# Windowed attention and a routed feed-forward: query tiles made of half blocks j and j+4

## The chip, the cores and the metric

One core of a Trainium2 chip runs the whole program. The metric is the device time of one execution in microseconds (us); the time before is the median of three runs, and one further execution was profiled.

## The reference, cut to what matters

Eight batches, eight heads, 576 positions, head dimension 64, all in float32. Each position looks at itself and the 127 positions before it, with a bias that grows with distance at a slope of the head's own. The attention's output goes, as 4608 rows of 512, through a mixture of eight experts of which each row uses two.

```python
scores = scale * np.matmul(q, k.transpose(0, 1, 3, 2))
rel = pos[:, None] - pos[None, :]
mask = (rel >= 0) & (rel < window)          # window = 128
scores = np.where(mask, scores + bias[None], -1000000000.0)
attn = np.exp(scores - np.max(scores, axis=-1, keepdims=True))
attn = attn / (np.sum(attn, axis=-1, keepdims=True) + 1e-09)
x = np.matmul(attn, v)                      # then rows (B * S, H * D)
...
noisy_logits = x @ w_gate + np.log1p(np.exp(x @ w_noise)) * noise
top2 = np.argpartition(-noisy_logits, 2, axis=1)[:, :2]
...
h = np.maximum(x[mask] @ w1[e], 0.0)
out[mask] += top2_w[mask, k, None] * (h @ w2[e])
```

## The kernel before

The program has two stretches. In the first, some 235 us, the attention of 32 pairs of heads (eight batches, four pairs each) is worked through, the rows are routed to experts, and the first expert's weights are made ready. In the second, the experts' two matrix products run on TensorE almost without a break, each as three float16 products of high and low halves.

A pair of heads is worked in units. Unit 0 takes query blocks 0 and 1 (of 128 rows), unit 1 takes blocks 2 and 3, and a third unit takes the half block 4 of two pairs at once. For each unit `unit` issues, one after the other, the following steps.

- `scores` on TensorE: in four quadrants of 64 by 64, the keys that a half block of 64 rows can see. They go to two PSUM banks of the ring `sb` (two such pairs of banks).
- `top` on VectorE: a row sees 128 keys that lie in two neighbouring key blocks. Since exactly one of the two keys at distance 128 is inside the window, `copy_predicated` (line 543) folds the two blocks of columns into one of 128, by the mask `own_key`. Block 0 has no block before it, so unit 0 folds 128 columns a head and unit 1 folds 256. Then one custom instruction for each block and head (line 535) adds the bias, writes `p` and the row's extreme `nm`.
- `soft` on ScalarE: the exponential (line 559), with the row sums.
- `trans` on TensorE (line 572): four transposes of 128 by 128 into one bank of the ring `tb`, against the identity; `evac` copies that bank to `pT` (line 274 on ScalarE, 278 on VectorE, whichever the planner takes).
- `split` on GpSimd (lines 592 and 593) undoes the fold in `pT` by two selections.

When both units of a pair are there, `weigh` (line 608) multiplies `pT` with the values into one bank of the ring `ob`, and `weighed` copies it to `xu`. When a batch is complete, `row_major` transposes `xu` back (line 754), divides by the row sums (line 757) and stores rows of `x` (line 762); `gate` and `route` find the experts and, in two large comparisons (line 886), the places. Lines 1381 to 1387 scale gathered rows for the first expert, lines 274, 276 and 1280 split its weights into high and low halves, and line 1416 is its first product. Line 531 and line 617 are scores and weighing of the third unit.

The order on each engine is no order of the source. Each step is a strand of a small simulation (`Order`) that runs when the program is built: it takes the step with the lowest rank whose inputs are there, charges it an assumed time, and so writes down each engine's queue. The constants at the top (`STAGE`, `LATE`, `TOP`, `WEIGHTS` and the others) are these ranks and assumed times; a copy that either of two engines could do goes to the one that is first free by them. On the chip each engine then runs its queue strictly in that order and waits on semaphores.

## Time and profile before

| | |
|---|---|
| median of three runs (lowest to highest) | 1017.89 us (1011.57 to 1019.82) |
| profiled execution, its own time | 1015.87 us |
| span in that profile, first to last instruction | 1014.1 us |
| TensorE busy | 963.3 us, 95% of the span |
| VectorE busy | 841.5 us, 83% |
| ScalarE busy | 562.2 us, 55% |
| GpSimd busy | 385.2 us, 38% |

The times of single steps come from the profiled execution. Its time is 1.8 us more than its span, and 2.0 us less than the median. Shares of the whole span mix the two stretches, so they have to be read stretch by stretch.

### The profile page before, as it was taken

How to read it: one execution, taken by the hardware profiler on the slowest of the kernel's cores; microseconds unless marked ns; L12 is line 12 of the kernel's file. 1: busy time of each engine (PE TensorE's matmuls, PEld its weight loads, DVE VectorE, ACT ScalarE, POOL GpSimd, SP SyncE). 2: the span in 40 equal slices, each digit the busy share in tenths (PEclk: the TensorE clock that was granted, in tenths of full speed). 3: DMA queues.
4: the chain of work that ended last, by engine and by line, in shares of the span. 5: the costliest groups of instructions: out<-in, count | busy, mean ns of one | idle time of the engine just before them, and what ended most of it. 6: DMA issues, size and time to landing. Idle time of an engine off the chain costs nothing. (4 is left out here: it accounts for less than half of the span.)

```text
span 1014.1 us, 24481 instructions
## 1 busy us (share of the span) xinstructions
PE 963.3 (95%) x8656; PEld 664.4 (66%) x8656; DVE 841.5 (83%) x2786; ACT 562.2 (55%) x1491; POOL 385.2 (38%) x572
## 2 busy tenths in 40 slices
PE   8999999979999999999999999899999999999996
PEld 5766666646555866686677567666766676667663
DVE  8999999998558989878999898769877897898530
ACT  8997797842136545445544556465556463554422
POOL 3557675864335122421343223232323231241103
PEclk9999999989999999999999999999999999999999
DMA  9887889643499999597868888769797896878113
GB/s 336 306 275 234 295 301 320 198 108 105 106 206 241 226 214 175 131 199 219 152 146 185 214 156 179 159 194 200 122 225 195 172 176 197 171 156 154 26 21 51
DMA packets 236333, 188.84 MB, mean 186 GB/s; under 512 B 147056, under 2 KB 190352, under 8 KB 236208
## 3 DMA queue, kind: packets, MB, share of 16 engines
q1 hardware_dynamic: 218864, 148.31, 56.6%
q0 software_dynamic: 17344, 38.94, 20.5%
q8 instruction: 69, 1.13, 0.5%
q14 instruction: 56, 0.46, 0.1%
HBM read 116.24 MB, written 40.71 MB: 155 GB/s over the span
## 5 line engine op out<-in xcount | busy, mean ns | idle before, releaser
L1677 POOL DMA_INDIRECT out_dram<-yo,ix x69 | 121.8, 1765 | 250.2 <-ACT yo L274 144.9
L1573 PEld LDWEIGHTS <-hh 128*128 128x128 f16 x896 | 87.3, 98 | 83.5
L1541 ACT ACTIVATE hh<-c 128x512 f16<-128x512 f32 (+1 forms) x103 | 53.4, 528 | 114.3 <-DVE c L1511 108.8
L1541 ACT ACTIVATE hh<-bank 128x256 f16<-128x256 f32 (+8 forms) x121 | 42.4, 352 | 130.2 <-PE bank L1416 61.3
L1290 POOL DMA_INDIRECT xg<-xs_dram,ix x34 | 41.7, 1225 | 182.0 <-DVE ix L1037 60.7
L1573 PE MATMUL bank<-w2ha,hh 128*128 128x512 f16 x288 | 109.2, 379 | 0.0
L1573 PE MATMUL bank<-w2la,hh 128*128 128x512 f16 x288 | 109.2, 379 | 0.0
L1573 PE MATMUL bank<-w2ha,hl 128*128 128x512 f16 x288 | 109.2, 379 | 0.0
L1442 PEld LDWEIGHTS <-wth 128*128 128x128 f16 x896 | 87.3, 98 | 25.0 <-issue 6.0
L559 ACT ACTIVATE p<-p,nm 128x128 f32<-128x128 f32 x256 | 99.5, 402 | 2.1 <-DVE nm L535 1.9
L1573 PEld LDWEIGHTS <-hl 128*128 128x128 f16 x448 | 43.8, 98 | 52.8
L1502 DVE TENSOR_TENSOR c<-bank,c 128x512 f32<-128x512 f32 x56 | 38.3, 684 | 41.3 <-PE bank L1442 40.7
L274 ACT ACTIVATE c<-bank 128x256 f32<-128x256 f32 x97 | 36.0, 379 | 58.3 <-PE bank L1442 53.3
L535 DVE CUSTOM_DVE_ANT_0 p<-bank,bias 128x128 f32<-128x128 f32 x288 | 66.7, 282 | 0.1
L1442 PE MATMUL bank<-xhw,wth 128*128 128x256 f16 x224 | 61.0, 272 | 4.3 <-DVE c L1502 2.8
L1290 POOL DMA_INDIRECT xp<-xs_dram,ix x35 | 38.4, 1096 | 66.5 <-issue 24.4
L592 POOL TENSOR_SCALAR_AFFINE_SELECT pT<-pT 128x256 f32<-128x256 f32 (+1 forms) x80 | 44.9, 562 | 44.8 <-ACT pT L274 36.8
L514 PE MATMUL bank<-qk 64*64 64x192 f32 (+1 forms) x1024 | 55.2, 330 | 6.7 <-DVE raw L355 4.6
L1442 PE MATMUL bank<-xhe,wth 128*128 128x256 f16 x224 | 61.1, 273 | 0.0
L1442 PE MATMUL bank<-xhe,wtl 128*128 128x256 f16 x224 | 61.1, 273 | 0.0
L1442 PE MATMUL bank<-xle,wth 128*128 128x256 f16 x224 | 61.1, 273 | 0.0
L1442 PE MATMUL bank<-xhw,wtl 128*128 128x256 f16 x224 | 61.0, 272 | 0.0
(339 smaller groups left out, 3162.0 us busy)
## 6 DMA issues: line engine op xcount, KB each, us to landing
raw<-in_w_dram SPq DMA_DIRECT2D x144, 256.0 KB
mraw<-in_w_dram SPq DMA_DIRECT2D x56, 512.0 KB
qk<-in_qk_dram SPq DMA_DIRECT2D x32, 576.0 KB
vraw<-in_v_dram SPq DMA_DIRECT2D x16, 640.0 KB
out_dram<-xg SPq DMA_DIRECT2D x10, 1024.0 KB
xs_dram<-x SPq DMA_DIRECT2D x32, 256.0 KB
out_dram<-yo,ix POOLq DMA_INDIRECT x69
xs_dram<-x SPq DMA_DIRECT2D x8, 128.0 KB
```

Of the source, the lines that this page charges most:

```text
L274: nc.scalar.activation(o, i, AF.Copy, **kw)
L514: nc.tensor.matmul(s[h][a:a + 64, o + first_:o + first_ + c_], qk[half, i * 128 + a:i * 128 + a + 64], qk[half, QW + k0 + first_:QW + k0 + ...
L535: nc.vector.tensor_tensor_reduce(out=o, in0=i, in1=by, scale=-0.125, scalar=3.0e38, op0=OP.add, op1=OP.min, accum_out=m)
L559: nc.scalar.activation(pv, pv, AF.Exp, bias=nm[:, z, h:h + 1], scale=-1.0, accum_out=den[:, i, 2 * g + h:2 * g + h + 1])
L592: nc.gpsimd.affine_select(b, a, pattern, OP.is_ge, nothing, base=0, channel_multiplier=-1)
L1290: nc.gpsimd.indirect_dma_start(out=o, out_offset=None, in_=xs[0:blk.rows], in_offset=bass.IndirectOffsetOnAxis(ap=blk.at[0:r, j:j + 1], ax ...
L1442: nc.tensor.matmul(t, wp[:, at + kc], xp[:, 2 * o + kc], start=not add and kc + z == 0, stop=kc + z == 3, skip_group_check=add)
L1502: yield dve(0.6, rank - MIDDLE, lambda: nc.vector.tensor_tensor(both, y, both, op=OP.add))
L1541: nc.scalar.activation(o, i, AF.Relu)
L1573: nc.tensor.matmul(blk.y[j], h[:, cs], wp, start=a == 0 and z + m == 0, stop=a == 3 and z + m == 3)
L1677: ins = nc.gpsimd.indirect_dma_start(out=out, out_offset=bass.IndirectOffsetOnAxis(ap=blk.ix[0:r, j:j + 1], axis=0), in_=t[0:r], in_offset ...
```

## The change

A query tile now holds two half blocks of 64 rows: half block j on partitions 0 to 63 and half block j+4 on partitions 64 to 127, for j from 0 to 3. Unit 0 takes tiles 0 and 1, unit 1 tiles 2 and 3; the third unit is unchanged. Each half block sees three half blocks of keys, of which only the first and the last share a place, so the fold is 64 columns a tile and head: 128 columns a head in both units. The bias has three ranges of columns in one tile of 320 instead of two tiles of 128 by head.

A unit no longer transposes by itself. `turning` waits for the exponentials of both units of a pair and takes two banks at once. It issues 16 transposes that read 64 partitions each, alternately the lower and the upper half, the lower half's into one bank and the upper half's into the other; so each bank comes out as two consecutive query blocks of 128, as `weigh` wants them. The buffers `p` of both units are freed together. `pT` has two buffers of a whole pair, and one small one for the third unit, where there were four.

The ring `tb` gets a third bank, and the ring `ob` keeps one. Because a tile's halves lie 256 rows apart, the store of `x` and of the gates becomes two transfers of 64 rows. The two tiles of the comparisons exist once instead of twice. All ranks and some assumed times have other values, so every queue is written anew.

On TensorE in the course of the attention, before: single units' transposes (line 572) stand between other work, one bank each. `p` and `pT` are the buffers named above, `vraw` the values, `qk` queries and keys.

```order
L514 MATMUL bank_69<-qk_80 64x192
L572 MATMUL bank_72<-ident,p_85 128x128 x4
L531 MATMUL bank_66<-qk_79 64x192
...
L608 MATMUL bank_70<-pT_97,vraw_84 64x256 x2
L608 MATMUL bank_70<-pT_97,vraw_84 64x128 x2
L608 MATMUL bank_70<-pT_98,vraw_84 64x256 x2
L608 MATMUL bank_70<-pT_98,vraw_84 64x128 x4
L617 MATMUL bank_71<-pT_99,vraw_84 64x64 x8
L572 MATMUL bank_73<-ident,p_86 128x128 x4
L572 MATMUL bank_72<-ident,p_87 128x128 x4
L514 MATMUL bank_68<-qk_81 64x128
```

After, at the like place (transposes are line 576, weighing line 613, scores line 523, the third unit's transposes line 580): the two units `p_87` and `p_88` are turned in one run of 16, alternating between two banks.

```order
L523 MATMUL bank_69<-qk_79 64x192
L613 MATMUL bank_70<-pT_96,vraw_84 64x4x64 x2
...
L613 MATMUL bank_70<-pT_96,vraw_84 64x2x64 x4
L576 MATMUL bank_72<-ident,p_87 128x64
L576 MATMUL bank_73<-ident,p_87 128x64
...
L576 MATMUL bank_72<-ident,p_88 128x64
L576 MATMUL bank_73<-ident,p_88 128x64
...
L576 MATMUL bank_72<-ident,p_87 128x64
...
L576 MATMUL bank_72<-ident,p_88 128x64
L576 MATMUL bank_73<-ident,p_88 128x64
L580 MATMUL bank_71<-ident,p_89 128x128 x2
L523 MATMUL bank_66<-qk_80 64x192
```

The transposes of a pair have moved together, behind the second unit's exponentials, and each takes half the columns.

On ScalarE, pairs five and six, before: copies of `pT` (line 274) stand between the exponentials (559, and 565 for the third unit), and so do the squares for the weights' sizes (line 1246).

```order
L274 ACTIVATE pT_96<-bank_73 128x4x128
L565 ACTIVATE p_89,denl_107<-p_89,nm_93 128x128 x2
L559 ACTIVATE p_85,den_105<-p_85,nm_94 128x128 x4
L274 ACTIVATE pT_97<-bank_72 128x2x128
L559 ACTIVATE p_86,den_105<-p_86,nm_95 128x128 x4
L559 ACTIVATE p_87,den_105<-p_87,nm_90 128x128 x4
L274 ACTIVATE pT_99<-bank_72 128x4x128
L559 ACTIVATE p_88,den_105<-p_88,nm_91 128x128 x4
L274 ACTIVATE pT_96<-bank_73 128x2x256
L1246 ACTIVATE raw_121,wam<-raw_121 128x512
L1246 ACTIVATE raw_122,wam<-raw_122 128x512
```

After, the same pairs (exponentials line 562, third unit 568, copies line 275):

```order
L562 ACTIVATE p_87,den_104<-p_87,nm_90 128x128 x4
L275 ACTIVATE pT_96<-bank_72 128x4x128
L275 ACTIVATE pT_96<-bank_71 128x4x128
L562 ACTIVATE p_88,den_104<-p_88,nm_91 128x128 x4
L568 ACTIVATE p_89,denl_107<-p_89,nm_92 128x128 x2
L562 ACTIVATE p_85,den_104<-p_85,nm_93 128x128 x4
L275 ACTIVATE pT_97<-bank_73 128x4x128
L275 ACTIVATE pT_97<-bank_72 128x4x128
...
L1291 ACTIVATE raw_120,wam<-raw_120 128x512
...
L275 ACTIVATE xu_100<-bank_70 128x512
L275 ACTIVATE pT_96<-bank_73 128x4x128
L275 ACTIVATE pT_96<-bank_72 128x4x128
```

All copies of `pT` stand on ScalarE now, both of a pair one behind the other; the squares come later.

On VectorE at the end of the attention, before: from the last main unit's `nm` (line 535) to the last unit's there stand both comparisons (line 886), three scaled tiles (line 1387) and others.

```order
L535 ISA nm_90 128x1
...
L1381 TENSOR_REDUCE fit_252<-xg 128x1
...
L1387 SCALAR_TENSOR_TENSOR th<-xg,fit_253,th 128x512
L886 TENSOR_TENSOR hot_197<-pl_193,steps 128x640
L1387 SCALAR_TENSOR_TENSOR th<-xg,fit_254,th 128x512
L886 TENSOR_TENSOR hot_196<-ln_192,steps 128x800
...
L757 TENSOR_TENSOR x_113<-bank_72,den_104 128x512
...
L551 COPY_PREDICATED bank_68<-own_key_129,bank_68 128x64
...
L535 ISA p_89,nm_91<-bank_68,bias_127 128x128
...
L535 ISA nm_91 128x1
...
L1280 SCALAR_TENSOR_TENSOR w1la_232<-raw_120,wsc,w1ha_231 128x512
```

After (line 538, comparisons line 923, scaled tiles line 1432, weights line 1325):

```order
L923 TENSOR_TENSOR hot_161<-pl_191,steps 128x640
...
L923 TENSOR_TENSOR hot_160<-ln_190,steps 128x800
...
L538 ISA nm_90 128x1
L1426 TENSOR_REDUCE fit_248<-xg 128x1
...
L785 TENSOR_TENSOR x_109<-bank_72,den_103 128x512
L1432 SCALAR_TENSOR_TENSOR th<-xg,fit_248,th 128x512
L1432 SCALAR_TENSOR_TENSOR th<-xg,fit_249,th 128x512
...
L554 COPY_PREDICATED bank_68<-own_key,bank_68 128x64
...
L538 ISA p_89,nm_91<-bank_68,bias_126 128x128
...
L538 ISA nm_91 128x1
...
L1325 SCALAR_TENSOR_TENSOR w2la_226<-raw_121,wsc,w2ha_225 128x512
...
L785 TENSOR_TENSOR x_112<-bank_73,den_104 128x512
```

The comparisons now stand ahead of the last main unit, the last unit's rows are nearer behind it, and parts of the weights follow them.

The diff, cut to its core:

```diff
-STAGE = (43.5, 39.9, 6.7, -53.5, -64.3, 730.4, 218.8, -21.0)
...
+STAGE = (191.6, 65.2, 12.9, -49.4, -203.3, 883.6, 669.6, -17.1)
...
-LATE = (37.9, -126.1, 327.0, 125.6, -510.9, -480.4, -2.7, -309.7, 117.8, 41.8, 62.0, -132.4, -374.6, -174.8, -14.4)
+LATE = (49.9, -308.2, 408.1, 325.6, -110.5, -347.4, -127.8, -366.9, 129.6, 46.8, 170.2, -73.5, -577.0, 45.9, 110.9)
...
-TOP, SOFT, SPLIT = (1.27, 1.52, 0.92), (1.56, 1.56, 0.8), (0.85, 1.35, 0.85)
...
+TOP, SOFT, SPLIT = (1.22, 1.22, 0.75), (1.56, 1.56, 0.8), (0.85, 1.35, 0.85)
...
-    ptr = ring(ap_, 4, [128, 2, 4, W], F32, "pT")
+    ptr = ring(ap_, 2, [128, 2, 2, 4, W], F32, "pT")
+    ptlr = ring(ap_, 1, [128, 2, 2, W], F32, "pTl")
...
-    sb, tb, ob = Ring([bank[0:2], bank[2:4]]), Ring([bank[7], bank[6]]), Ring([bank[4], bank[5]])
+    sb, tb, ob = Ring([bank[0:2], bank[2:4]]), Ring([bank[7], bank[6], bank[5]]), Ring([bank[4]])
...
+    def blocks_of(v, first_, step, n_):
+        return bass.AP(tensor=v.tensor, offset=v.offset + first_ * 64, ap=[list(v.ap[0]), [step * 64, n_], [1, 64]])
...
+    def scores(k, g, s):
         qk = qks[k]
-        for z, i in enumerate(blocks):
-            k0, c = (i - 1) * 128 if i else 0, width(i)
-            o = place_of(blocks, z)
-            for a in (0, 64):
-                first_, c_ = (a, c - 64) if i else (0, c)
-                for h in range(2):
-                    half = slice(h * D, h * D + D)
-                    nc.tensor.matmul(s[h][a:a + 64, o + first_:o + first_ + c_], qk[half, i * 128 + a:i * 128 + a + 64],
-                                     qk[half, QW + k0 + first_:QW + k0 + first_ + c_], start=True, stop=True)
-    def width(i):
-        return (128, 256, 256, 256, 192)[i]
-    def place_of(blocks, z):
-        return sum(width(i) for i in blocks[:z])
+        for z in range(2):
+            for r in range(2):
+                m = 2 * g + z + 4 * r
+                if z == 0:
+                    lst = ((0, 3, m - 2 if m else 0, 1 if m else 0),)
+                elif m == 1:
+                    lst = ((192, 2, 1, -1), (320, 1, 0, 1))
+                else:
+                    lst = ((192, 3, m, -1),)
+                for o, n_, first_, step in lst:
+                    for h in range(2):
+                        half = slice(h * D, h * D + D)
+                        nc.tensor.matmul(s[h][r * 64:r * 64 + 64, o:o + n_ * 64], qk[half, m * 64:m * 64 + 64],
+                                         blocks_of(qk[half, QW:QW + S], first_, step, n_), start=True, stop=True)
...
-    def top(k, blocks, s, p, nm):
-        g = k % NP
-        z0 = blocks[0] == 0
+    def top(k, g, s, p, nm):
         for h in range(2):
-            sv = s[h][:, 128 * z0:512 - 128 * z0].rearrange("p (z a c) -> p z a c", a=2, c=W)
-            nc.vector.copy_predicated(sv[:, :, 0], own_key.bitcast(U32)[:, None, :].to_broadcast([128, 2 - z0, W]), sv[:, :, 1])
-        for z, i in enumerate(blocks):
-            o = place_of(blocks, z)
+            fold = bass.AP(tensor=s[h].tensor, offset=s[h].offset, ap=[list(s[h].ap[0]), [320, 2], [1, 64]])
+            nc.vector.copy_predicated(fold, own_key.bitcast(U32)[:, None, :].to_broadcast([128, 2, 64]),
+                                      s[h][:, 128:256].rearrange("p (z c) -> p z c", z=2))
+        for z in range(2):
+            at = (64, 0)[z] + 128 * (g == 0)
             for h in range(2):
-                biased_and_largest(p[:, z, h], s[h][:, o:o + W], bias[:, int(i == 0), 2 * g + h], nm[:, z, h:h + 1])
+                biased_and_largest(p[:, z, h], s[h][:, z * 256:z * 256 + W], bias[:, 2 * (k % NP) + h, at:at + W],
+                                   nm[:, z, h:h + 1])
...
-    def trans(p, t, nh):
+    def trans(ps, ts):
+        for n in range(8):
+            h, j = n // 4, n % 4
+            for r in range(2):
+                rows_ = slice(r * 64, r * 64 + 64)
+                nc.tensor.transpose(ts[r][:, n * 64:n * 64 + 64], ps[j // 2][rows_, j % 2, h], ident[rows_, rows_])
...
-    def evac(e, blocks, t, pt):
-        if blocks == (4,):
-            copy(e, pt[:, :, 0], t[:, 0:2 * W].rearrange("p (h c) -> p h c", h=2))
-        else:
-            copy(e, pt[:, :, 0:2] if blocks[0] == 0 else pt[:, :, 0:4:2], t.rearrange("p (h z c) -> p h z c", h=2, z=2))
+            nc.tensor.transpose(t[:, z * W:z * W + W], p[:, z, 0], ident)
+    def evac(e, r, t, pt):
+        copy(e, pt[:, r].rearrange("p h (i s) c -> p (h i) s c", s=2)[:, :, 0], t.rearrange("p (n c) -> p n c", c=W))
...
     def weigh(k, blocks, pt, o):
-        t = values_[k // 2]
-        if blocks[0] == 0:
-            lst = [(0, 0, 0, 0), (1, 1, 2, 128)]
-        else:
-            lst = [(blocks[0], 0, 1, 0), (blocks[0] - 1, 1, 0, 0), (blocks[0] + 1, 1, 3, 128)]
-        for m, (kb, one_, at, o0) in enumerate(lst):
+        t, g = values_[k // 2], blocks[0] // 2
+        lst = ([(0, slice(0, 4, 2), 0), (1, slice(3, 4), 1)] if g == 0 else
+               [(2, slice(1, 3), 0), (1, slice(0, 1), 0), (3, slice(3, 4), 1)])
+        for m, (kb, at, i0) in enumerate(lst):
             for h in range(2):
                 half, hh = slice(h * D, h * D + D), (k % 2 * 2 + h) * D
-                c = 128 if one_ else 256
-                w = pt.rearrange("p h s c -> p h (s c)")[:, h, at * 128:at * 128 + c]
-                nc.tensor.matmul(o[half, o0:o0 + c], t[:, kb, hh:hh + D], w, start=m == 0, stop=m == len(lst) - 1)
+                w = pt[:, g, h, at].rearrange("p i (z c) -> p i z c", z=2)
...
+    softened = [(Event(2), []) for _ in range(PAIRS)]
+    both_banks = Ring([0])
...
+        yield pe(0.24, r3, lambda: trans_of_last(p, a))
         put(pr, p)
-        yield either(*((0.29, 0.33) if last else (0.48, 0.6)), r4, LATE[3], lambda e: evac(e, blocks, a, pt))
+        yield either(0.29, 0.33, r4, LATE[3], lambda e: evac_last(e, a, pt))
         put(tb, a)
         yield pool(SPLIT[gr], r5, lambda: split(blocks, pt))
-        if not last:
-            parts[k, gr] = pt
-            mark(parted[k])
-            mark(over)
-            return
         yield valued[y]
         o = yield (ob, r6)
         yield pe(0.5, r6, lambda: weigh_last(k, pt, o), mode="columns")
-        put(ptr, pt)
+        put(ptlr, pt)
         yield from weighed(b, g, t, 1, r7, o[:, 0:128].rearrange("p (z c) -> p z c", z=2), o)
+        mark(over)
+    def turning(k):
+        r3, r4, r5 = (k * NQ + 1 + z for z in STAGE[3:6])
+        yield softened[k][0]
+        ps = [p for _, p in sorted(softened[k][1], key=lambda x: x[0])]
+        pt = parts[k] = yield (ptr, r3)
+        yield (both_banks, r3)
+        ts = []
+        for _ in range(2):
+            ts.append((yield (tb, r3)))
+        yield pe(0.6, r3, lambda: trans(ps, ts), mode="rows")
+        for p in ps:
+            put(pr, p)
+        for r in range(2):
+            spawn(out_of_bank(k, r, ts[r], pt, r4, r5))
+        put(both_banks, 0)
+    def out_of_bank(k, r, t, pt, r4, r5):
+        yield either(0.48, 0.6, r4, LATE[3], lambda e: evac(e, r, t, pt))
+        put(tb, t)
+        yield pool(SPLIT[r], r5, lambda: split(GROUPS[r], pt))
+        mark(parted[k])
         mark(over)
...
+                weigh(k, GROUPS[gr], parts[k], o)
         yield pe(1.58, r6, both_groups, mode="columns")
-        for gr in range(2):
-            put(ptr, parts[k, gr])
+        put(ptr, parts[k])
         yield from weighed(b, g, t, 0, r7, o, o)
...
-        yield from move(2.6e5, rank, lambda: nc.sync.dma_start(
-            dram(xs, (b * S + i * 128) * XW, [[XW, rows], [1, DM]]), x[0:rows]))
+        def store():
+            if i == 4:
+                nc.sync.dma_start(dram(xs, (b * S + 512) * XW, [[XW, 64], [1, DM]]), x[0:64])
+                return
+            for r in range(2):
+                nc.sync.dma_start(dram(xs, (b * S + (4 * r + i) * 64) * XW, [[XW, 64], [1, DM]]),
+                                  x[r * 64:r * 64 + 64])
+        yield from move(2.6e5, rank, store)
...
+    hotr = Ring([[ap_.tile([128, 2 * NQ, c], F16, name=f"hot{c}") for c in (E * SPAN, LINE)]])
...
+            yield based[b - 1]
...
-            yield based[b - 1]
...
+        hot = yield (hotr, rank)
...
+        put(hotr, hot)
...
-        for _ in range(2):
-            t = yield (ob, 0)
+        for r in (ob, tb):
```

## Rows read from the trace of the kernel before

**Rows 1.** Stretches of the span: engines' busy us (instructions), granted clock, DMA share.

```profile
core 0: us, PE busy (x) PEld busy (x) DVE busy (x) ACT busy (x) POOL busy (x), PEclk, DMA share, GB/s
...
70.00:213.00 143.00, 133.92 (x1873) 93.20 (x1864) 137.98 (x747) 115.50 (x477) 104.60 (x212) 1.00 0.78 256
213.00:231.70 18.70, 14.34 (x118) 8.80 (x117) 16.23 (x44) 6.02 (x16) 12.46 (x23) 0.73 0.40 95
...
250.00:600.00 350.00, 338.48 (x2501) 233.15 (x2499) 293.81 (x773) 171.40 (x326) 112.75 (x115) 1.00 0.86 184
600.00:1004.70 404.70, 394.34 (x3147) 273.41 (x3145) 310.70 (x779) 197.67 (x381) 114.39 (x118) 1.00 0.73 152
```

**Rows 2.** Stretches of the attention, the same columns.

```profile
20.00:40.00 20.00, 20.00 (x290) 14.56 (x290) 19.59 (x99) 20.00 (x90) 9.09 (x19) 1.00 0.90 310
40.00:60.00 20.00, 19.48 (x289) 13.32 (x291) 19.62 (x121) 20.00 (x90) 9.88 (x20) 1.00 0.88 297
...
160.00:200.00 40.00, 37.60 (x552) 25.97 (x549) 38.83 (x203) 30.54 (x133) 27.72 (x59) 1.00 0.80 275
```

**Rows 3.** Groups by line on VectorE, 0:240 us: busy us, mean ns | idle before.

```profile
L535 DVE CUSTOM_DVE_ANT_0 p<-bank,bias 128x128 f32<-128x128 f32 x288 | 66.7, 282 | 0.1
L543 DVE COPY_PREDICATED bank<-own_key,bank 128x256 f32<-128x256 uint32 x64 | 23.9, 418 | 0.2
...
L543 DVE COPY_PREDICATED bank<-own_key,bank 128x128 f32<-128x128 uint32 x64 | 15.4, 284 | 1.7 <-PE bank L514 1.7
...
L278 DVE COPY pT<-bank 128x512 f32<-128x512 f32 x9 | 6.1, 679 | 0.3 <-PE bank L572 0.3
...
L1387 DVE SCALAR_TENSOR_TENSOR th<-xg,fit,th 128x512 f16<-128x512 f32 x3 | 2.7, 904 | 0.0
...
L1381 DVE TENSOR_REDUCE fit<-xg 128x1 f32<-128x512 f32 x3 | 2.0, 679 | 0.0
```

**Rows 4.** The same view on ScalarE.

```profile
L559 ACT ACTIVATE p<-p,nm 128x128 f32<-128x128 f32 x256 | 99.5, 402 | 2.1 <-DVE nm L535 1.9
L559 ACT ACTIVATION_READ_ACCUMULATOR p<-p,nm 128x1 f32 x256 | 51.7, 202 | 0.0
L274 ACT ACTIVATE pT<-bank 128x512 f32<-128x512 f32 x55 | 32.0, 594 | 7.7 <-PE bank L572 3.6 <-DVE nm L535 2.0 <-ACT u L834 0.9
```

**Rows 5.** The same view on TensorE.

```profile
L572 PE MATMUL bank<-ident,p 128*128 128x128 f32 x288 | 47.2, 287 | 6.1 <-ACT pT L274 2.7 <-DVE x L757 1.8 <-ACT p L559 0.5
L514 PE MATMUL bank<-qk 64*64 64x192 f32 x768 | 46.8, 340 | 0.4 <-DVE nm L535 0.4
L608 PE MATMUL bank<-pT,vraw 128*64 128x256 f32 x256 | 41.2, 400 | 0.1
```

**Rows 6.** Timeline of TensorE near 208 us: start us, us, engine, line.

```profile
207.38 0.64 PE L572 MATMUL bank<-ident,p 128*128 128x128 f32 x4
...
208.44 0.69 PE L617 MATMUL bank<-pT,vraw 128*64 128x64 f32 x16
```

**Rows 7.** Timeline of VectorE at the attention's end.

```profile
208.81 0.28 DVE L535 CUSTOM_DVE_ANT_0 p<-bank,bias 128x128 f32<-128x128 f32 x1
...
217.06 1.25 DVE L886 TENSOR_TENSOR hot<-pl,steps 128x640 f16<-128x640 int32 x1
...
218.90 2.04 DVE L886 TENSOR_TENSOR hot<-ln,steps 128x800 f16<-128x800 int32 x1
...
223.62 0.28 DVE L535 CUSTOM_DVE_ANT_0 p<-bank,bias 128x128 f32<-128x128 f32 x1
...
225.03 0.74 DVE L1280 SCALAR_TENSOR_TENSOR w1la<-raw,wsc,w1ha 128x512 f16<-128x512 f32 x1
```

**Rows 8.** Timeline of TensorE there.

```profile
225.25 0.66 PE L572 MATMUL bank<-ident,p 128*128 128x128 f32 x2 [0.24 <-issue]
...
231.74 0.34 PE L1416 MATMUL bank<-xhe,w1ha 128*128 128x384 f16 x1
```

**Rows 9.** Line 762, the stores of x: min/median/max ns.

```profile
L762 SPq DMA_DIRECT2D xs_dram<-x x40: 319/403/1590, 35.9 to 241.1; - x40
```

More of the change, by code (lines that the diff above doesn't have):

```diff
@@ L24 @@
 QW = S
+BW = 320
 GROUPS = ((0, 1), (2, 3), (4,))
@@ L644, in unit @@
         mark(seated)
-        yield pe((0.66, 0.77, 0.43)[gr], r0, lambda: scores_of_last(k, s) if last else scores(k, blocks, s),
+        yield pe((0.66, 0.77, 0.43)[gr], r0, lambda: scores_of_last(k, s) if last else scores(k, gr, s),
                  mode="quads")
@@ L1021, in gates_out, with store @@
         yield pool(1.1, rank, gates_)
-        for i0, ni, rows in ((0, 4, 128), (4, 1, 64)):
-            yield from move(2e4, rank, lambda: nc.sync.dma_start(
-                dram(xs, (b * S + i0 * 128) * XW + DM, [[XW, rows], [128 * XW, ni], [1, E]]), gd[0:rows, i0:i0 + ni]))
+        def store():
+            for r in range(2):
+                nc.sync.dma_start(dram(xs, (b * S + 256 * r) * XW + DM, [[XW, 64], [64 * XW, 4], [1, E]]),
+                                  gd[r * 64:r * 64 + 64, 0:4])
+        yield from move(2e4, rank, store)
+        yield from move(2e4, rank, lambda: nc.sync.dma_start(
+            dram(xs, (b * S + 512) * XW + DM, [[XW, 64], [XW, 1], [1, E]]), gd[0:64, 4:5]))
         mark(sent[b])
```

116 lines of the change are left out of this document (61 added, 55 removed).

## The prediction

> **What bounds the kernel now.** I read the engines' busy time by stretches first, because shares of the whole span mix two programs. From 250 us to 1004.7 us TensorE is busy for 338.48 of 350 us and 394.34 of 404.7 us [rows 1]: the experts' products are bound by TensorE and leave it 22 us idle in all. The change touches no product there. What it can win must be won before the first expert product at 231.74 us [rows 8], and what it does to the queues can move only those 22 us behind it.
>
> Within the attention the bound changes. From 20 to 60 us ScalarE is busy for 20.00 of every 20 us, VectorE for 19.59 and 19.62 [rows 2]. A pair of heads costs ScalarE eight exponentials, (99.5 + 51.7) / 32 = 4.7 us, and most of its copies of 0.594 us [rows 4]. From 70 to 213 us VectorE is the bound with 137.98 of 143 us; ScalarE has 115.50, TensorE 133.92 [rows 1], and the window from 160 to 200 us reads alike [rows 2]. The start, about 12 of the 32 pairs (I place the change-over near 68 us, where ScalarE ceases to be full), is thus ScalarE's; the other 20 pairs are VectorE's. Last comes a tail: from the last main unit's bias and extreme at 208.81 us to the last unit's at 223.62 us VectorE is busy [rows 7], and the first product waits for what follows from that.
>
> **The fold.** It was two instructions of 256 columns and two of 128 a pair; now it is four of 128. By busy time, which counts overlaps once, the wide kind costs 23.9 / 64 = 0.373 us and the narrow 15.4 / 64 = 0.241 us [rows 3]. The saving on VectorE is 64 x 0.132 = 8.5 us. The narrow kind now reads its 128 columns as two pieces of 64; no row shows that form. Bounds: as a plain 128 (0.241), or as dear as a 256 (0.373), saving nothing. I take 0.241: the count of elements made the difference between the two known forms, and the wide one was already cut in two.
>
> **Copies of pT.** VectorE made nine, of 0.679 us [rows 3]; in the new order it makes one, and ScalarE 63 instead of 55. That takes 8 x 0.68 = 5.4 us off VectorE and lays 8 x 0.594 = 4.8 us [rows 4] on ScalarE. After 70 us ScalarE has 27 us to spare [rows 1], which hides it; before 60 us it has nothing, and a copy more there is a delay in full. By counting the queue up to pair 12's exponentials, with each row at its group's mean, ScalarE ends up with 1 us less there, not more, because squares for the weights stand later.
>
> **Other work on VectorE.** Two more copies of weighted values come to it (as dear as a pT copy, +1.4 us), and the two comparisons, 1.25 and 2.04 us [rows 7], are moved ahead of the last main unit, +3.3 us there. So up to the last main unit VectorE's work changes by -8.5 - 5.4 + 1.4 + 3.3 = -9.2 us.
>
> **What of that is kept.** In the first 12 pairs VectorE loses 12/32 of 13.9 us, 5.2 us; but ScalarE stays full there, and only its own -1 us counts. VectorE may use the rest by running ahead, yet only as far as the five `p` buffers let it, about one pair. For the other 20 pairs it keeps 20/32 of 13.9 = 8.7 us, against 1.4 + 3.3 us added: -4.0 us. Together -5 by that count. The bounds are -1 (all but ScalarE's part is lost to waits between engines, since a pair's transposes now wait for both units) and -9.2 (the five buffers pass everything on). I take **-4 us**: the window of 160 to 200 us leaves VectorE 1.17 us in 40 unfilled [rows 2], so near 3% of any gain there is lost, and the longer wait costs something more.
>
> **The transposes.** A pair had two runs of four, 0.64 us each [rows 6], 1.28 us. With 0.287 us for one alone [rows 5], the next follows after (0.64 - 0.287) / 3 = 0.118 us. Now 16 stand in one run, each on 64 rows and with half the columns out. No row shows this form. The cheapest neighbour is the third unit's weighing, 16 small products in 0.69 us [rows 6]; the dearest price is full intervals for each, 15 x 0.118 + 0.287 = 2.05 us. Between -0.59 and +0.77 us a pair, I take -0.2 us (a lower and an upper half share one interval: 7 x 0.118 + 0.287 = 1.11 us), because the quadrant products of `scores`, which also lie on row halves, last 0.340 us each but cost 46.8 / 768 = 0.061 us of busy time [rows 5], so several run at once. The gain falls on an engine with 9 us to spare in 143 and counts nothing. Behind the run on TensorE stand the next scores; they are delayed if the second unit's exponentials are late, and that wait is in the -4 above.
>
> The Trainium skill, page "TensorE: Matmul & The Clock Gate", section "LDWEIGHTS (loading the stationary operand)", speaks against this edit: a load's time goes with its columns, not with its rows, so 16 half loads would cost twice 8 whole ones. By that alone a run would cost the 2.05 us above, and the time would be the slower rival's below. The part on packing small matmuls on the same page says that loads overlap matmuls in flight when the row groups differ, which by itself would give 1.11 us and leave my sum as it is. No row here shows which holds for a load of 128 columns on 64 rows.
>
> **Banks and stores.** One bank for weighted values instead of two: a pair's weighing must wait until the pair before has been copied out (about 0.6 us, the price of a copy [rows 4]). Where weighings stand apart by more than that, nothing is late. In the order some 8 of 47 stand close together: at most 8 x 0.6 = 4.8 us on TensorE, which has that much idle time; I take 0, with 4 us for the upper end. The stores add 40 issues of 0.403 us [rows 9], 16 us spread over SP's queue for 200 us; nobody waits for single stores except the gather of the first tokens, where one more issue is 0.4 us.
>
> **The tail.** Out of the 14.8 us between the two units' extremes [rows 7] go the comparisons, 3.3 us, and one of three scaled tiles with its reduction, 0.904 + 0.679 us [rows 3]: -4.9 us. But five pieces of weights of 0.74 us [rows 7] now stand behind the last unit, ahead of the last rows of `x`; TensorE's last transposes, 225.25 us, follow the last unit at once, and 6.5 us more pass until the first product [rows 8]. Charged in full the pieces are +3.7 us, charged to idle time 0; VectorE is busy for 16.23 of these 18.7 us [rows 1], but some pieces stood there before too. I take +1, so the tail gives **-4 us**, with bounds -5 and -1. The granted clock there is 0.73 with TensorE busy for 14.34 us [rows 1]; at full clock it would need 3.9 us less, at 1.2 GHz throughout some 6.6 us more (14.34 x 0.73 / 0.5 - 14.34). I take no change.
>
> **The second stretch.** Its idle 22 us are drawn anew, since all ranks are new. Nothing says which way; I charge 0, with 6 us to either side, about a quarter of them.
>
> **Sum.** -4 - 4 = -8 us. Against the profiled execution's 1015.87 us that is 1007.9; the runs' median is 2.0 us higher, the same -8 from there is 1009.9. I say 1009.
>
> **Rivals.**
> 1. *Everything is kept.* The queues pass on VectorE's whole -9.2 us, and the shorter tail holds TensorE busy enough for the full clock: -9.2 - 4.9 - 3.9 = -18, or 998; with half of the last two terms 1002. For it: VectorE, not ScalarE, is the bound of the longer part. Against it: 40 us with ScalarE at 20.00 of 20.
> 2. *Nothing is kept.* The full ScalarE and the wait for both units swallow the -4, the weights' pieces and 4 us of stalls in the second stretch the tail: 0 to +2, so 1016 to 1020. For it: a unit's transposes no longer follow its own exponentials, and the buffers of `p` come free two at a time. Against it: after 70 us three engines have room.
> 3. *Slower.* The row halves don't overlap, and the run costs 2.05 us, +0.77 a pair. In the first 12 pairs, where TensorE reads 20.00 and 19.48 of 20 us busy, that is +9.2 us; in the other 20 it is 15.4 us against the 9.1 us that TensorE has free, +6.3. Less the tail's 4: +11.5, so 1029. It decides from the point where a run takes over 1.28 + 9.1 / 20 = 1.73 us. The concurrent quadrants speak against it.
>
> **How the numbers follow.** This kernel's times lie 8 us apart before any change, so 1%, 10 us, is about what can be told from none. The forecast (1003 to 1014) has a chance of 0.45, rival 1 0.22, rival 2 0.2, rival 3 0.13. Faster by over 1%, below 1007.7 us: all of rival 1 and a third of the forecast, 0.37. Slower, above 1028: most of rival 3, 0.1. Within 1%: 0.53. The range runs from 999 us, which leaves out the best of rival 1, to 1023 us, which takes in rival 2 and leaves out rival 3.
>
> **What would show it.** In the new profile: folds all near 0.24 us busy each, VectorE some 9 us less busy before the last main unit, which ends near 204 to 205 us; ScalarE still full from 20 to 60 us; a run of 16 transposes near 1.1 us; the last unit some 8 us behind the last main unit, and the first expert product near 223 to 224 us; idle TensorE time in the second stretch within 6 us of 22. The prediction is wrong if the attention's pairs don't get closer after 70 us, if the run costs over 1.7 us, or if the second stretch changes by more than the attention does.

## The result and the profile after

The changed kernel takes 1000.66 us (median of four runs, 999.62 to 1001.41) against 1017.91 us; the ratio is 0.9841, 95% interval 0.9804 to 0.9878. Its profiled execution took 1000.38 us, 15.5 us less than that of before. The forecast was 1009 us with a range of 999 to 1023: direction and range held, but the gain is twice what was summed, and it did not come from where the sum had it.

Windows of the changed kernel (same columns as [rows 1]); the window of 760.10 us is from the first expert product to TensorE's last instruction:

```profile
0.00:207.50 207.50, 188.20 (x3103) 139.58 (x3105) 192.37 (x1098) 182.73 (x750) 137.63 (x300) 0.99 0.85 280
20.00:40.00 20.00, 20.00 (x359) 15.60 (x353) 19.06 (x103) 20.00 (x93) 10.77 (x22) 1.00 0.76 259
40.00:60.00 20.00, 19.49 (x348) 14.20 (x348) 18.16 (x115) 20.00 (x81) 8.81 (x19) 1.00 0.95 325
...
70.00:211.00 141.00, 126.77 (x2102) 93.76 (x2104) 134.58 (x768) 120.29 (x483) 106.44 (x215) 0.97 0.84 270
211.00:228.50 17.50, 14.89 (x137) 10.06 (x134) 15.60 (x45) 6.71 (x18) 14.90 (x25) 0.73 0.48 93
...
228.52:988.62 760.10, 749.61 (x5792) 517.71 (x5791) 616.84 (x1622) 374.26 (x723) 230.64 (x248) 1.00 0.81 169
250.00:600.00 350.00, 342.76 (x2531) 237.14 (x2530) 292.95 (x770) 179.46 (x342) 107.70 (x113) 1.00 0.89 185
```

The two stretches of before that answer to the first and to the 760.10 us:

```profile
0.00:208.90 208.90, 195.73 (x2726) 135.82 (x2727) 200.59 (x1088) 177.72 (x740) 134.18 (x292) 1.00 0.83 278
...
231.74:1004.74 773.00, 751.02 (x5805) 518.44 (x5800) 620.82 (x1636) 373.71 (x718) 235.23 (x254) 1.00 0.78 166
```

TensorE's idle time after the first expert product fell from 773.00 - 751.02 = 22.0 us to 760.10 - 749.61 = 10.5 us. That is 11.5 of the 15.4 us that the span lost; 1.4 us is TensorE's busy time there, and 0.7 us was given back behind its last instruction. Only 3.2 us come from the attention: the first product starts at 228.52 us, before at 231.74 us [rows 8].

VectorE and TensorE by line in the changed kernel, 0:240 us and 0:245 us:

```profile
L544 DVE COPY_PREDICATED bank<-own_key,bank 128x128 f32<-128x128 uint32 x128 | 30.7, 283 | 2.3 <-PE bank L523 2.0
...
L279 DVE COPY pT<-bank 128x512 f32<-128x512 f32 x1 | 0.7, 673 | 0.0
```

```profile
L576 PE MATMUL bank<-ident,p 64*128 64x64 f32 x512 | 24.8, 235 | 2.7 <-DVE listed L940 2.2 <-ACT p L562 0.5
L580 PE MATMUL bank<-ident,p 128*128 128x128 f32 x32 | 6.8, 293 | 0.0
```

A fold costs 30.7 / 128 = 0.240 us, the price of the old narrow kind [rows 3]. The run of 16 transposes costs 24.8 / 32 = 0.78 us a pair; all transposes together 31.6 us against 47.2 [rows 5], 15.6 us less of TensorE.

The end of the attention: the last main unit and the last unit on VectorE, then GpSimd, then TensorE.

```profile
207.27 0.28 DVE L538 CUSTOM_DVE_ANT_0 p<-bank,bias 128x128 f32<-128x128 f32 x1
...
214.74 0.28 DVE L538 CUSTOM_DVE_ANT_0 p<-bank,bias 128x128 f32<-128x128 f32 x1
...
210.80 1.53 POOL L1008 DMA_INDIRECT slots_dram<-listed,line_of  x1 [3.86 <-DVE listed L940]
212.37 0.40 POOL L599 TENSOR_SCALAR_AFFINE_SELECT pT<-pT 128x256 f32<-128x256 f32 x1
...
219.97 2.63 POOL L600 TENSOR_SCALAR_AFFINE_SELECT pTl<-pTl 128x256 f32<-128x256 f32 x1
...
222.66 0.69 PE L622 MATMUL bank<-pTl,vraw 128*64 128x64 f32 x16 [1.98 <-POOL pTl L600]
...
228.52 0.32 PE L1461 MATMUL bank<-xhe,w1ha 128*128 128x384 f16 x1
```

Against [rows 7] the last main unit is 1.5 us earlier (207.27 for 208.81) and the last unit 8.9 us (214.74 for 223.62). But from there to the first product it is now 13.8 us, before 8.1. GpSimd stood for 3.86 us ahead of an indirect store, with the selections of the last pairs queued behind it; the last of them, 2.63 us long, lets TensorE's last weighing wait 1.98 us.

TensorE's largest waits within 70:211 us of the changed kernel (us in total, times, longest):

```profile
PE bank L932 <- POOL hot L928: 4.3, 4, 2.2
PE bank L576 <- DVE listed L940: 2.2, 1, 2.2
PE bank L932 <- DVE hot L923: 2.1, 1, 2.1
```

These 8.6 us are waits for the routing's comparisons and for what follows from them; in the kernel before TensorE waits 0.2 us for these from 70 to 213 us.

### The profile page after: what moved, and what is told of

It reads as the page before. It is cut to its first block, busy times and chain, and to the rows that moved or that the text cites. A ratio compares the mean times of both kernels' runs of the same rounds, so it can differ in the third digit from the quotient of the medians.

```text
span 998.7 us, 25321 instructions
## 1 busy us (share of the span) xinstructions
PE 954.0 (96%) x9040; PEld 668.4 (67%) x9040; DVE 828.1 (83%) x2776; ACT 567.1 (57%) x1500; POOL 384.8 (39%) x574
## 5 line engine op out<-in xcount | busy, mean ns | idle before, releaser
L1586 ACT ACTIVATE hh<-bank 128x256 f16<-128x256 f32 (+8 forms) x126 | 44.4, 354 | 138.3 <-PE bank L1461 92.7
L1335 POOL DMA_INDIRECT xp<-xs_dram,ix x35 | 41.6, 1189 | 178.9 <-ACT hh L1586 45.0
L1586 ACT ACTIVATE hh<-c 128x256 f16<-128x256 f32 (+1 forms) x101 | 51.3, 520 | 95.0 <-DVE c L1556 91.5
L523 PE MATMUL bank<-qk 64*64 64x192 f32 (+2 forms) x1152 | 59.6, 330 | 7.3 <-DMA qk<-in_qk_dram 4.7
L1291 ACT ACTIVATE mraw<-mraw 128x1024 f32<-128x1024 f32 x56 | 58.6, 1046 | 8.8 <-DMA mraw<-in_w_dram 8.5
L1487 PE MATMUL bank<-xlw,wth 128*128 128x256 f16 x224 | 61.0, 272 | 0.0
L1618 PE MATMUL bank<-w2hb,hh 128*128 128x512 f16 x160 | 60.6, 379 | 0.0
```

What stands on the lines that cost most here:

```text
L523: nc.tensor.matmul(s[h][r * 64:r * 64 + 64, o:o + n_ * 64], qk[half, m * 64:m * 64 + 64], blocks_of(qk[half, QW:QW + S], first_, step, n_) ...
L1291: yield act(us, rank, lambda: nc.scalar.activation(v, v, sum_, accum_out=o))
L1335: nc.gpsimd.indirect_dma_start(out=o, out_offset=None, in_=xs[0:blk.rows], in_offset=bass.IndirectOffsetOnAxis(ap=blk.at[0:r, j:j + 1], ax ...
L1487: nc.tensor.matmul(t, wp[:, at + kc], xp[:, 2 * o + kc], start=not add and kc + z == 0, stop=kc + z == 3, skip_group_check=add)
L1586: nc.scalar.activation(o, i, AF.Relu)
L1618: nc.tensor.matmul(blk.y[j], h[:, cs], wp, start=a == 0 and z + m == 0, stop=a == 3 and z + m == 3)
```

## The experiments

The first product's start and the idle time behind it (window less TensorE's busy time, as above) tell in every run which stretch a change has moved. Ratios are to the kernel before, whose median was 1014.7 to 1015.3 us beside these runs (the changed kernel's is to 1017.9). The changed kernel was not timed again beside them, so a difference to its 1000.7 us can be off by some 3 us, as the kernel before moved. First product and idle time come from one profiled execution each (e2's was the slowest of its four, 1032.6 us). How far chance moves the first product can be told from e9, e10 and e12: their queues up to it are those of the kernels that they come from, and it starts 0.65 to 0.74 us later.

| run | us, ratio [interval] | first product | idle behind it |
|---|---|---|---|
| before | 1017.9 | 231.7 | 22.0 |
| changed | 1000.7, 0.984 [0.980, 0.988] | 228.5 | 10.5 |
| e1 changed, old ranks of stretch two | 1042.3, 1.027 [1.025, 1.030] | 237.4 | 32.1 |
| e2 before, new ranks of stretch two | 1026.3, 1.009 [1.006, 1.012] | 231.2 | 27.8 |
| e3 changed, all old ranks | 1026.9, 1.011 [1.009, 1.013] | 234.2 | 27.6 |
| e4 before, all new ranks | 1074.6, 1.057 [1.055, 1.060] | 232.3 | 64.4 |
| e5 changed, 64 folds more | 1018.1, 1.003 [1.001, 1.005] | 245.5 | 11.9 |
| e6 changed, transposes twice | 1009.7, 0.994 [0.992, 0.996] | 236.6 | 13.0 |
| e7 before, fold cut | 1013.9, 1.000 [0.997, 1.002] | 230.1 | 21.3 |
| e8 before, fold and transposes cut | 1039.2, 1.023 [1.021, 1.025] | 225.6 | 17.7 |
| e9 before, gathers +4 us | 1030.0, 1.014 [1.010, 1.019] | 232.4 | 29.8 |
| e10 before, gathers +2 us | 1021.3, 1.005 [1.003, 1.007] | 232.5 | 24.2 |
| e11 changed, halves in two blocks | 1006.9, 0.992 [0.989, 0.995] | 232.8 | 13.5 |
| e12 changed, gathers +4 us | 1015.1, 1.000 [0.998, 1.001] | 229.2 | 21.7 |

**Layout or numbers (e1 to e4).** The new layout came with new ranks, so both were exchanged. In e1 these lines of the changed kernel get the old values, with `MIDDLE`, `RESULT`, `SIZES`, `SOON` and `BEHIND` likewise; e2 puts the new values into the kernel before. e3 and e4 exchange all ranks (all but `TOP`).

```diff
-FFN0, FFN1 = 143.9, 256.9
-WEIGHTS = (351.6, 286.6)
-TOKENS = 503.7
+FFN0, FFN1 = 159.1, 159.3
+WEIGHTS = (164.0, 310.1)
+TOKENS = 270.3
...
-PACE, READ_BY, AHEAD = 0, 2.0, 85.9
+PACE, READ_BY, AHEAD = 0.3, 2.0, 16.1
```

> The changed kernel with the old ranks of the second stretch alone (FFN0, FFN1, WEIGHTS, TOKENS, MIDDLE, RESULT, SIZES, SOON, BEHIND, PACE, AHEAD); layout and attention ranks stay new. In the changed kernel the first expert product starts only 3.2 us earlier (228.5 us), but TensorE's idle time from there on fell from 22.0 to 10.5 us. Theory A, the gain is for the most part the new ranks of the second stretch: its idle time returns to some 20 us and the time to 1009 to 1013 us. Theory B, the gain comes from the layout, which relieves VectorE and TensorE and lets the weights for the later experts be made earlier: the time stays within 3 us of 1001.

> The kernel before with the new ranks of the second stretch alone. Theory A (the ranks of the second stretch make the gain): idle time of TensorE after the first expert product near 10 us instead of 22, the time 1004 to 1008 us. Theory B (the layout makes it): within 4 us of the kernel before's 1018.

> The changed kernel with all of the old ranks (the assumed time of the folds, TOP, stays new): the layout alone. Theory A: 1010 to 1016 us, with some 20 us of idle time in the second stretch; Theory B: 1000 to 1005 us. By my sum for the attention alone, whoever is right about the second stretch, the first expert product should start 3 to 8 us before the old 231.7 us.

> The kernel before with all of the new ranks: the numbers alone, without the layout. Theory A: 1004 to 1009 us, for the idle time of the second stretch goes with its ranks; Theory B: 1014 to 1022 us, and the start of the first expert product not earlier than 231 us.

Neither theory fits: all four are slower than both kernels. Ranks that serve one layout are poor for the other, so these runs don't divide the gain; but they show that the second stretch's idle time (27.6 to 64.4 us) goes its own way. The most telling is e3, the layout in the old ranks. VectorE's last unit and the first product there, by the timelines of the two engines:

```profile
198.65 0.29 DVE L538 CUSTOM_DVE_ANT_0 p<-bank,bias 128x128 f32<-128x128 f32 x1
...
234.24 0.53 PE L1461 MATMUL bank<-xhe,w1ha 128*128 128x384 f16 x1
```

All units are through 25 us earlier than before (198.65 for 223.62 us), and yet the first product is 2.5 us later, where I expected it 3 to 8 us earlier. Most of the 25 us isn't the layout: VectorE has done 183.8 us of work when it gets to its last unit, in the kernel before 214.7, because routing, scaled tiles and weights now stand behind the pairs, and there TensorE waits 6.0 us at one place and 4.2 us at another. Up to the first product VectorE does 8.0 us less than before (212.6 for 220.6), about what the lighter layout saves.

**The worth of the lighter engines, order unchanged (e5 to e8).** e5 and e6 repeat work in the changed kernel whose results are the same. e7 leaves one of unit 1's two folds out in the kernel before, e8 also half of the main units' transposes from the twelfth unit on.

```diff
-            nc.vector.copy_predicated(fold, own_key.bitcast(U32)[:, None, :].to_broadcast([128, 2, 64]),
...
+            for _ in range(2 if g == 0 else 1):
+                nc.vector.copy_predicated(fold, own_key.bitcast(U32)[:, None, :].to_broadcast([128, 2, 64]),
...
```

```diff
-        for n in range(8):
+        for n in list(range(8)) * 2:
```

```diff
-            nc.vector.copy_predicated(sv[:, :, 0], own_key.bitcast(U32)[:, None, :].to_broadcast([128, 2 - z0, W]), sv[:, :, 1])
+            nc.vector.copy_predicated(sv[:, 0:1, 0], own_key.bitcast(U32)[:, None, :].to_broadcast([128, 1, W]), sv[:, 0:1, 1])
```

```diff
-        for z in range(2):
+        turned.append(nh)
+        for z in range(2 if nh == 1 or len(turned) < 12 else 1):
             for h in range(nh):
```

> The changed kernel with the two folds of unit 0 issued twice (the second writes the same values): 64 instructions more on VectorE, 64 x 0.24 = 15.4 us, 1.8 times what the folds of the layout saved, every queue otherwise in the same order. Theory C, the work that the layout takes off the attention is worth its time where it lies on the bound of a pair: the first expert product comes 9 to 15 us later than 228.5 us and the time rises by as much, to 1009 to 1016 us, with the idle time after that product still near 10.5 us. Theory D, VectorE isn't what paces the attention any more and the gain is the order alone: less than 3 us later, 1001 to 1004 us.

> The changed kernel with the 16 transposes of a pair issued twice: 24.8 us more on TensorE (1.6 times what the halves saved against the old form, 15.6 us), same order otherwise. If TensorE has room beside VectorE, as I argued in the prediction, only what goes over its idle time counts (9 us from 70 to 200 us, none before): the first product 8 to 16 us later, 1009 to 1017 us. If the halves' saving was worth nothing at all: below 3 us. If TensorE is the bound throughout: some 25 us, 1025 us.

> The kernel before with unit 1's fold cut to one of its two blocks (the other block's fold is left out, so some rows see wrong keys): 64 instructions of 256 columns become 128, 8.5 us less on VectorE, all queues in the old order. Theory C: the first product 3 to 7 us before 231.7 us, the idle time behind it still 18 to 26 us, the time 1009 to 1014 us. Theory B of the first call, that a lighter attention takes the second stretch's stalls away: idle time near 10 us and a time below 1006 us. Theory D: no change in the first product.

> As the run before, and from the twelfth unit on two of a main unit's four transposes are left out too (the copies then carry old values): some 110 transposes less, 13 us of TensorE, about what the row halves save. With both, the kernel before has the layout's lighter engines in its own order. Theory C: the first product 5 to 10 us earlier than 231.7, idle time behind it unchanged at 18 to 26 us, time 1006 to 1012 us. Theory B: idle time near 10 us. If transposes count for nothing, the same as the run before within 2 us.

The folds of e5 from 0 to 250 us, and the window behind its first product:

```profile
L545 DVE COPY_PREDICATED bank<-own_key,bank 128x128 f32<-128x128 uint32 x192 | 49.7, 289 | 4.4 <-PE bank L523 2.1
...
245.50:1008.70 763.20, 751.28 (x5792) 518.05 (x5791) 616.29 (x1620) 374.10 (x723) 228.90 (x248) 1.00 0.80 168
```

The 64 folds cost 49.7 - 30.7 = 19.0 us of VectorE, not the 15.4 that I had said (a repeated one takes 0.297 us). They moved the first product by 17.0 us and the time by as much, above my range; the idle time behind it stayed (11.9 us). So work added to VectorE counts for 0.9 of itself in the changed order, although VectorE is idle for 15.1 of its first 207.5 us there: that idle time isn't room. The fold also stands in the chain of each unit, from scores to exponentials; whether the engine's queue or that chain makes the cost was not separated. The transposes twice, in e6:

```profile
L576 PE MATMUL bank<-ident,p 64*128 64x64 f32 x1024 | 42.3, 235 | 2.7 <-DVE listed L940 2.7
```

17.5 us more of TensorE (the doubled run costs less than twice the single one, where I had said 24.8) moved the first product by 8.1 us, 0.46 of it.

In the old order the same relief is worth less: in e7 8.5 us off VectorE brought the first product forward by 1.6 us only, twice what chance does and below the 3 to 7 that I expected, and the time is the same. With the transposes' 11.7 us off TensorE as well (35.5 us in place of 47.2), e8's first product comes 6.1 us earlier: the transposes are worth 4.5 us, more than the folds. After its last regular product e8 does work that the others don't have, because rows with wrong values are routed otherwise; its time is therefore not compared, only what lies before:

```profile
L575 PE MATMUL bank<-ident,p 128*128 128x128 f32 x178 | 35.5, 296 | 8.9 <-ACT pT L274 5.1 <-DVE x L760 1.9 <-DVE bank L551 0.4
```

```profile
225.60:995.20 769.60, 751.95 (x5808) 518.98 (x5800) 620.57 (x1636) 374.71 (x718) 233.51 (x255) 1.00 0.78 167
```

```profile
1011.34 0.87 PE L1929 MATMUL ot<-ident,oxg 128*128 128x128 f32 x3 [16.06 <-DMA owa<-in_w_dram]
```

Its idle time, 769.60 - 751.95 = 17.7 us, is nearer to the old 22.0 than to the new 10.5, and e7's is 21.3. A lighter attention takes at most 4.3 of the 11.5 us away (and e8's rows are routed otherwise, which was not separated); a heavier one (e5, e6) brings 2.5 us back at most. For the most part the stalls go with the order.

**What the stalls are (e9, e10, e12).** In the kernel before, VectorE's timeline and TensorE's at the second stretch's longest stall but one:

```profile
298.66 0.68 DVE L1381 TENSOR_REDUCE fit<-xp 64x1 f32<-64x512 f32 x1 [3.48 <-DMA xp<-xs_dram,ix]
...
301.63 0.41 DVE L1543 TENSOR_SCALAR hh<-bank 128x256 f16<-128x256 f32 x1
```

```profile
302.62 0.27 PE L1416 MATMUL bank<-xhe,w1ha 128*128 128x256 f16 x1 [1.84 <-DVE hh L1543]
```

VectorE's queue stands for 3.48 us at a reduction whose rows a gather has not yet brought; the evacuation of a bank is queued behind it, and TensorE waits 1.84 us for that bank. VectorE's waits for gathers in the second stretch of before and of the changed kernel, the largest rows:

```profile
DVE fit L1381 <- DMA xg<-xs_dram,ix: 12.6, 4, 4.0
DVE fit L1381 <- DMA xp<-xs_dram,ix: 4.3, 3, 3.5
```

```profile
DVE xp L1377 <- DMA xp<-xs_dram,ix: 0.8, 3, 0.3
DVE fit L1426 <- DMA xp<-xs_dram,ix: 0.5, 1, 0.5
```

The 16.9 us of these two kinds (line 1381 before, 1426 after) had become 0.5; with line 1332 before and 1377 after, 18.1 us had become 1.3. (For the first expert's rows, gathered by `cl`, they are 1.4 and 2.3 us.) That looked like the cause, and it could be tried without touching the attention, by one assumed time, set at two places of the planner (2 and 4 us more in the kernel before, 4 in the changed one):

```diff
-        yield max(order.now + 3.4, at)
+        yield max(order.now + 3.4, at) + 4.0
...
-        yield max(order.now + 3.4, order.transfer(order.now, 2048.0 * r))
+        yield max(order.now + 3.4, order.transfer(order.now, 2048.0 * r)) + (0 if blk in first else 4.0)
```

> The kernel before, with one assumed time changed: gathered rows of the later blocks are taken to land 4 us later, so that the order places what VectorE does with them later. The queues of the attention stay as they were. In the kernel before four of TensorE's longest waits in the second stretch, 7.4 us in all, stand right behind a wait of VectorE for such a gather (3.5, 1.2, 3.9 and 4.0 us), with the evacuation of a bank queued behind it. Theory E, the second stretch's stalls are these blocked evacuations: VectorE's waits for gathered rows fall below 3 us in all, TensorE's idle time from 22 to 14 to 17 us, the time by 5 to 8 us. Theory F, every new order is a new draw: the waits may go, but the idle time falls anywhere between 15 and 35 us.

> The same with 2 us instead of 4. Theory E: between the kernel before and the run with 4 us, idle time 16 to 21 us; Theory F: no relation to the run with 4 us.

> The changed kernel with the gathers of the later blocks taken to land 4 us later, as a control: in its second stretch VectorE waits for no gathered rows where TensorE stands. Theory E: nothing to win, 999 to 1004 us. Theory F: a new draw, idle time anywhere from 8 to 25 us and a time up to 1015 us.

VectorE's waits for transfers in the second stretch of e9, and TensorE's largest:

```profile
DVE yo L276 <- DMA out_dram<-yo,ix: 6.8, 3, 5.0
...
DVE fit L1381 <- DMA xg<-xs_dram,ix: 0.7, 1, 0.7
```

```profile
PE bank L1442 <- DVE c L1502: 11.9, 8, 3.1
```

The waits for gathers are all but gone, yet 6.8 us of waiting for stores of results have come in their place (0.6 us before), and the idle time rose from 22.0 to 29.8 us; other evacuations (line 1502) are late. e10 has 24.2 us. In the changed kernel, which had no such waits to lose, the same edit took the idle time from 10.5 to 21.7 us. Theory E falls. F fits, with its wide ranges, but it isn't shown against a third reading, that placing these steps later costs by itself: with 0, 2 and 4 us the idle time is 22.0, 24.2 and 29.8 us, and no run took the time shorter. The head-of-line waits explain single stalls of before, but moving them away is no remedy by itself: the new order has others.

Seven other orders (e1 to e4, e9, e10, e12) gave 21.7 to 64.4 us. The changed kernel's 10.5 is the lowest of all, and it is worth most of the gain; why just this order stalls so little stays open. The seven aren't draws of one kind: e1 to e4 mix ranks of one kernel with the layout or the ranks of the other, and 29.8 of e4's 64.4 us are one wait of an expert's first product for its rows, at 360 us. Its window and that wait:

```profile
232.30:1062.70 830.40, 765.97 (x5923) 527.86 (x5922) 623.69 (x1650) 385.43 (x753) 245.21 (x271) 0.97 0.75 156
...
PE bank L1416 <- DMA xhe<-th: 29.8, 1, 29.8
```

Idle time also understates what the slowest orders cost. In e1, e2, e4 and e9 TensorE is busy for 6.6 to 15.0 us longer behind the first product than in the kernel before (751.02 us at a granted clock of 1.00), at a mean granted clock of 0.97 to 0.99, and in e4 with 118 matmuls more.

**The halves' alternation (e11).**

```diff
-        for n in range(8):
-            h, j = n // 4, n % 4
-            for r in range(2):
+        for r in range(2):
+            for n in range(8):
+                h, j = n // 4, n % 4
```

> The changed kernel with the 16 transposes of a pair issued as eight of the lower half and then eight of the upper, not alternately; count, columns and banks are the same. If neighbours on different row halves share their time (the reason for the alternation), a pair's run, now 24.8 / 32 = 0.78 us, goes up to between 1.1 and 2.05 us, 10 to 40 us more of TensorE in all, and by the slope of the doubled transposes (8.1 us later for 24.8) the time rises by 3 to 13 us. If each costs what its own 64 columns cost, the run and the time stay as they are.

```profile
L576 PE MATMUL bank<-ident,p 64*128 64x64 f32 x512 | 34.9, 235 | 1.6 <-DVE listed L940 1.5 <-ACT p L562 0.2
```

Eight and eight cost 34.9 / 32 = 1.09 us a pair, alternately 0.78 us. So neighbours on different row halves share time. The 10.1 us of TensorE brought the first product from 228.5 to 232.8 us and the time to 1006.9 us. Of the 6 us that the alternation is worth by the time, 4.3 lie in the attention; the idle time behind the first product rose by 3.0 us too, and why was not tried. The slope in the expectation took e6's doubling at 24.8 us; with the 17.5 that it cost, the 10 to 40 us would have meant 5 to 19.

## Why the prediction held in its range and was short in its size

- **The bound** was read rightly in part. ScalarE is still full from 20 to 60 us while VectorE fell to 19.06 and 18.16 of 20. But VectorE isn't the only bound after 70 us: in the old order 8.5 us off it gave 1.6 us (e7). That the transposes' saving "counts nothing" is a step that failed: a us of transposes is worth 0.38 us (4.5 for 11.7, e8 against e7), 0.43 (4.3 for 10.1, e11) or 0.46 (e6). Rival 3 had charged the same time in full in the first 12 pairs, so the sum was at odds with it.
- **The single prices** were right: the fold at 0.24 us, one copy of `pT` left on VectorE, VectorE's work up to the last main unit -8.2 us (192.37 for 200.59) where I summed -9.2. The run of 16 came out at 0.78 us, below the 1.1 that I took and within the bounds; rival 3 needed over 1.73 us.
- **What of that is kept: -4 us** was too much; the last main unit came 1.5 us earlier, and VectorE's idle time up to there grew from 8.3 to 15.1 us. The exponentials of the main units show where (the last one of the first 12, the first 28 and all 32 pairs; before, then after):

```profile
68.74 0.39 ACT L559 ACTIVATE p<-p,nm 128x128 f32<-128x128 f32 x1
...
182.90 0.40 ACT L559 ACTIVATE p<-p,nm 128x128 f32<-128x128 f32 x1
...
211.38 0.39 ACT L559 ACTIVATE p<-p,nm 128x128 f32<-128x128 f32 x1
```

```profile
67.33 0.42 ACT L562 ACTIVATE p<-p,nm 128x128 f32<-128x128 f32 x1
...
175.88 0.40 ACT L562 ACTIVATE p<-p,nm 128x128 f32<-128x128 f32 x1
...
208.13 0.39 ACT L562 ACTIVATE p<-p,nm 128x128 f32<-128x128 f32 x1
```

They are 1.4, 7.0 and 3.2 us earlier. The first 12 pairs gave what I said (1 us), and pairs 13 to 28 kept 5.6 of the 7.0 us that my 13.9 give for 16 pairs. The last four gave 3.8 us back. Between them VectorE now has six rows of `x` where there were two (line 785 for 757, 3.9 us for 1.4), three pieces of the weights (line 1325, 2.2 us for none) and more comparisons (line 923 for 886, 4.9 us for 3.8); I had charged +3.3 for comparisons, and nothing for the others. I also left one edit uncosted: the comparisons' new place and single tiles, where TensorE now waits 8.6 us. Whether the single tiles or the order causes that was not tried.
- **The tail: -4 us**, measured -1.7. Its first half gave more than I said (the units' distance fell from 14.8 to 7.5 us, -7.3 for my -4.9). The second half cost +5.7 us where I charged +1: I had looked at VectorE's pieces of weights, and by the waits the chain went over GpSimd's queue, which I had not followed; no run took that wait away. The granted clock there is 0.73 as before.
- **The second stretch: 0, within 6 us to either side.** This is the term that failed: -11.5 us of idle time. I had written that nothing says which way, but a quarter of 22 us was far too narrow: the seven other orders spread from 21.7 to 64.4 us, all but one above the old 22.0.

By its own sign ("if the second stretch changes by more than the attention does", here 11.5 us against 3.2) the prediction's mechanism was wrong, and that the time lies in its range is to that extent luck. With the attention's 3.2 us alone it would be near 1015 us, an estimate, which that wide range holds as well. The total lies near rival 1's 1002 us (counted from the profiled execution, while rival 3 counts from the median, 2 us higher), but not by its mechanism: rival 1 took it from VectorE's saving kept whole and the full clock, and neither happened.

Shown are: the second stretch's gain goes for the most part with the order (e5 to e8), work of the kind that the layout saves costs time in the new order (e5, e6, e11), and the layout with the old ranks is slower than the kernel before (e3). By e5's slope (17.0 for 19.0) the folds' 8.5 us would be worth some 7.6 us at the new order, and by e6's and e11's the transposes' 15.6 us some 7, both estimates. If these slopes held for work taken off as well, the new order would cost the attention elsewhere some 11 us, for the first product came only 3.2 us earlier; e7 says that they need not hold. e8, with both reliefs in the old order, has its first product at 225.6 us. Open is whether as good an order for the second stretch could be had with the old layout.

The Trainium skill, page "TensorE: Matmul & The Clock Gate", section "LDWEIGHTS (loading the stationary operand)", would price 16 half loads at twice eight whole ones. For the single load the traces agree: 0.141 us with 128 rows before, 0.143 us with 64 rows after, each of 128 columns (rows of the loads, 0:240 us).

```profile
L572 PEld LDWEIGHTS bank<-ident,p 128*128 128x128 f32 x288 | 30.8, 141 | 22.3 <-ACT p L559 6.5 <-ACT pT L274 5.0 <-issue 3.0
```

```profile
L576 PEld LDWEIGHTS bank<-ident,p 64*128 64x128 f32 x512 | 19.8, 143 | 9.1 <-DVE listed L940 2.4 <-issue 2.0 <-ACT p L562 1.2
```

The price of a run doesn't follow from it, because the loads overlap: 16 of 0.143 us would be 2.29 us one after the other, but the 16 took 1.09 us even in two blocks, against 1.28 us for the two old runs [rows 6]. Alternately they took 0.78 us, which agrees with the page's part on packing small matmuls, by which loads overlap matmuls in flight when the row groups differ.

## What to carry to other kernels

Where a planner writes the queues, a change of layout and its ranks are one change: test the layout with doses at a fixed order (repeat an operation whose result stays the same), and treat the rest of the program as a new order whose spread is measured, not guessed. Read a dose's cost from the trace, too: the same fold cost 0.240 us once and 0.297 us more when repeated. An engine's idle time in a chain of units that wait on one another is no room: 19.0 us of added work cost 17.0 us on an engine that stood idle for 7% of the stretch. But such a dose doesn't price a relief: 8.5 us less on the same engine, in the old order, gave 1.6 us. A stall that disappears together with a gain need not be its cause: take it away alone before believing it.

## What was not expected of the hardware

Sixteen float32 transposes of 64 rows take 0.78 us when lower and upper halves alternate, and 1.09 us in two blocks of eight, although nothing but their sequence differs. And TensorE's granted clock fell inside the attention, to 0.66 of full speed from 100 to 105 us, after a stretch in which TensorE had been busy for 2.46 of 5 us:

```profile
95.00:100.00 5.00, 2.46 (x40) 1.91 (x41) 4.89 (x17) 0.49 (x2) 4.62 (x8) 1.00 0.60 112
100.00:105.00 5.00, 4.78 (x72) 3.66 (x71) 4.49 (x30) 4.23 (x20) 4.26 (x8) 0.66 0.85 236
...
102.00:103.00 1.00, 1.00 (x15) 1.00 (x19) 1.00 (x9) 1.00 (x7) 1.00 (x2) 0.50 0.83 283
```

The 0.66 is a mean of the two levels; from 102 to 103 us it was the lower one, 1.2 GHz. In the kernel before it was 2.4 GHz throughout 70 to 200 us. What the slower microseconds cost in time no run shows.
